# Sums of inputs for Strassen products in five steps, first group's products reordered, spectral split a row later

## The chip, the cores and the metric

One Trainium2 chip, of which the kernel uses one core. A core has engines with instruction queues of their own: TensorE (PE; its weight loads are shown as PEld), VectorE (DVE), ScalarE (ACT), GpSimd (POOL) and SyncE (SP), which here issues most of the transfers; 16 DMA engines move the data. The metric is device time in microseconds (us) of one execution, lower is better. Times are compared as medians of several runs.

## The reference

Two branches read the same layer-normalised input, and their sum is added to the input:

```python
x = A_u                                  # (1, 2048, 576)
xn = _layernorm(x, axis=-1)
return x + _A_ref(xn, ...) + _B_ref(xn, B_w1, B_w2)

# _A_ref: a state-space convolution over the sequence
logdA = dt * A;  dB = dt * Bc
P = jnp.exp(logdA[:, :, None] * l[None, None, :])
K = jnp.einsum("dn,dnl,dn->dl", Cc, P, dB).real     # 576 kernels of length 2048
...
Yf = Uf * Kf[None, :, :, :]                         # product of the two spectra
y = ... irfft ... + u * Dskip[None, None, :]

# _B_ref: a feed-forward layer, F = 4608
h = _silu(jnp.einsum("bsd,df->bsf", x, w1))
out = jnp.einsum("bsf,fd->bsd", h, w2)
```

## The kernel before

**Numbers.** Matrix products run on float32 values that are split into a high and a low part (names ending in h and l): three products, high by high, high by low and low by high, stand for one. The splits are a cast on ScalarE (h) and a subtraction on VectorE (l). An inner dimension of 576 is four tiles of 128 and a rest of 64, whose high and low parts share one tile of 128 rows (x4, x40, x41).

**The feed-forward branch** (`ffn`) sets the order of the program. The sequence has four blocks of 512 tokens, two to a half. A first matmul with w1 (`up`) makes 128 hidden features by 512 tokens, `gate`-like code applies SiLU and splits the result into gh and gl, and `down` multiplies 128 tokens of it with w2 into PSUM tiles po of 288 columns, which VectorE adds into the accumulators acc (L313). The first half, and two chunks of the second half, run block by block in that way (up to L418).

**The Strassen part** (`wino_ffn`, L421) does the rest of the second half. A group n (14 of them, `first` to `end`) is 256 hidden features (f = 2n and 2n + 1) by both blocks of 512 tokens, with the inner dimension halved into 2 x 256: a 2 x 2 by 2 x 2 product, made of seven products rather than eight, in the form with shared sums. `prod` is one such product, six matmuls of 512 columns; `rest` adds the rest of the inner dimension, two matmuls. On the weight side sums are made per group (`sums`, `prep`, `split`), named c1, c2, t13 and t24. On the input side they are made once, by `wino_x` (L548):

- `join` puts the halves of x together again (x21, x22, x11, x12: VectorE, 128 x 1024 each);
- S1 = x21 + x22, S2 = S1 - x11, S3 = x11 - x21, S4 = x12 - S2, each split by `parts` (ScalarE, then VectorE). S3 overwrites the tiles of x21's block;
- d4 is the difference of the two rests (tiles e and d).

A[0], A[1] and A22 are parts of the input that need no sum. `wino_x` makes S1, S2, S4 and d4, yields once, and makes S3.

In a group the PSUM tiles are pb (name pb or pb2), pc (`ps_c`) and pa (`ps_a`): c1·A[0] goes to pb and is copied to pa; t13·S1 and a rest go to pc, copied to the SBUF tile f5; t24·S2 is added on pb, and VectorE makes pc = pb + f5 (L504); t13·S3 is added on pb, and f5 = pb + f5 (L510). Then come two ends: `lower` (the gate of f5, the product t24·A22 on pb and its gate) and `upper` (c2·S4 on pc with its gate, c1·A[1] on pa with its gate). Which end runs first alternates with n, since the next group's `down` steps d[0] to d[3] need the block whose gates came first. Between the products stand the previous group's `down` steps and the weights' loads and splits (`second`, `prep`).

**The convolution branch** runs as a side program (`side`), woven into the main one: `weave` counts the main program's yields (276 steps) and lets the side program go on whenever the count has reached the fraction that it last yielded. First come the kernel's taps (`kgen`, up to 0.613), stored to d1k, then `wino_x` at 0.6215, then `spectral` between 0.6215 and marks[2] = 0.855, then `tail`. `spectral` has 32 rows. `front(k)` loads the row of the input (ur) and of the kernel (kr), splits both, multiplies each with a Fourier matrix (pu, pk), forms the complex product ka (VectorE, with copies by ScalarE, L870 to L879) and splits it to yh and yl (`split_of`); in the loop, `front(k + 1)` stands ahead of the last product of row k (tile pb of L892, from yh and yl), which is copied to yo and stored to d2. The memory of the kernel's taps (pool of `stage`), of `wino_x`'s sums and of the spectral rows is used one after the other.

**The end.** The convolution's output for 128 tokens (`add_conv`, tiles py) needs rows of d2 from all 32 spectral rows, so that its loads (ys, 32 of them) can begin only when the last row is stored; six of them are buffered at a time. r holds the first half's result, stored earlier in dr0 and loaded again; after the addition (L971) it is stored (L172).

**Who sets the order.** The text gives a priority by its order, and a scheduler with a time model of its own orders each engine's queue at build time; what is inside `high_priority` goes ahead, `behind(ins)` keeps an instruction after another of its engine. At run time each engine works its queue strictly in that order, and waits at the first instruction whose inputs or buffers are not ready. The lines that the change touches are L486 to L541 (the group), L548 to L588 (`wino_x`), L852 to L895 (`spectral`) and L1018 to L1024 (the fractions).

Of the kernel before, what the change touches and what calls it, by code (L numbers as in the profile page):

```python
# [41 lines left out]
def kernel(  # L42
# [21 lines left out]
    nc = tc.nc  # L64
# [25 lines left out]
    s4 = None  # L90
# [39 lines left out]
    xts = {}  # L130
    pairs = {}
    pins = {}
    wino = {}
# [287 lines left out]
    def wino_ffn(load_w1, load_w2, split_w2, prep, WT, first, end, W2, before, down):  # L421

        ps_a = ps1.tile([P, 512], F32, tag="ps1", name="pa")
        ps_c = ps1.tile([P, 512], F32, tag="ps1", name="pc")
        A, A22, S1, S2, S3, S4, x40, x41, d4 = wino["x"]
        nc.tensor.matmul(ps_a, x40[:, :P], x40, start=True, stop=True)
        G = {}

        def unit(name, n, a):
            h, l = WT[name, n]  # L430
            return h[:, a:a + 2], l[:, a:a + 2]

        def prod(dst, w, x, start=False, stop=False):
            (wh, wl), (xh, xl) = w, x
            n = 0
            for a, v in ((wh, xh), (wh, xl), (wl, xh)):
                for kt in range(2):
                    pins["pe"] = nc.tensor.matmul(dst, a[:, kt], v[:, kt], start=start and n == 0, stop=stop and n == 5,  # L438
                                                  skip_group_check=True).ins
                    n += 1  # L440

        def rest(dst, name, n, at, x4, stop=True):
            for i in range(2):
                pins["pe"] = nc.tensor.matmul(dst, WT[name, n][i][:, at], x4, start=False, stop=stop and i == 1,
                                              skip_group_check=True).ins

        def gate(src, b, f):
            gf = gp.tile([P, 512], F32, tag="gf", name="gf", bufs=2)
            spare = len(G) % 6 == 5
            gh, gl = ((wino["pool"] if spare else gp).tile([P, 512], F32R, tag=n, name=n) for n in ("gh", "gl"))  # L450
            G[b, f] = gh, gl
            with tc.high_priority():
                nc.scalar.activation(gf, src, AF.Silu)
                pins["gh"] = nc.scalar.copy(gh, gf).ins
                pins["gl"] = nc.vector.tensor_sub(gl, gf, gh).ins

        def load(n):
            if n < end:
                load_w1(1, n // 2, n % 2 * 2)

        def second(n, i, part):
            if first <= n < end:
                f = 2 * n + i
                (load_w2 if part == "load" else split_w2)(1, f // FT, f % FT)

        load(first + 1)
        for i in range(2):
# [12 lines left out]

        def run_of(b, ns):
            fs = [2 * n + i for n in ns for i in range(2)]
            blk = (1, NCH - 1 if ns[-1] == end - 1 else WINO_C, b)
            return [lambda jj=jj: down(blk, jj, [(G[b, f], W2[1, f // FT, f % FT]) for f in fs]) for jj in range(4)]

        for n in range(first, end):  # L486
            d = downs(n - 1)
            pb = ps2.tile([P, 512], F32, tag="ps2", name="pb2")
            f5 = wino["pool"].tile([P, 512], F32, tag="f5", name="f5", bufs=1)
            prod(pb, unit("c1", n, 0), A[0], start=True)  # L490
            with tc.high_priority():
                nc.scalar.copy(ps_a, pb)
            prod(ps_c, unit("t13", n, 0), S1, start=True)
            rest(ps_c, "c2", n, 2, x41)
            with tc.high_priority():
                nc.scalar.copy(f5, ps_c)
            yield 0
            d[0]()
            second(n, 0, "split")
            second(n + 1, 0, "load")  # L500
            yield 0
            prod(pb, unit("t24", n, 0), S2)
            with tc.high_priority():
                nc.vector.tensor_add(ps_c, pb, f5)  # L504
            d[1]()
            prep(n + 1, "c2")
            yield 0
            prod(pb, unit("t13", n, 2), S3)
            with tc.high_priority():
                nc.vector.tensor_add(f5, pb, f5)  # L510
            d[2]()
            prep(n + 1, "c1")
            prep(n + 1, "sums")
            yield 0
            d[3]()
            second(n, 1, "split")
            second(n + 1, 1, "load")
            yield 0

            def lower():  # L520
                gate(f5, 1, 2 * n + 1)
                prod(pb, unit("t24", n, 2), A22)
                gate(pb, 1, 2 * n)

            def upper():
                prod(ps_c, unit("c2", n, 0), S4)
                rest(ps_c, "c2", n, 2, d4)
                gate(ps_c, 0, 2 * n + 1)
                prod(ps_a, unit("c1", n, 2), A[1])
                rest(ps_a, "c1", n, 4, x40)  # L530
                gate(ps_a, 0, 2 * n)

            rest(pb, "c1", n, 4, x41, stop=False)
            for k, f in enumerate((lower, upper) if n % 2 == 0 else (upper, lower)):
# [12 lines left out]

    def wino_x(sx, xp):  # L548

        (ah, al, x40), (bh, bl, x41) = xts[2], xts[3]  # L550

        def join(h, l, k, name):
            t = sx.tile([P, 2, 512], F32, name=name)
            nc.vector.tensor_add(t, h[:, k:k + 2].bitcast(F32), l[:, k:k + 2].bitcast(F32))
            return t

        def parts(src, h, l):
            with behind(pins["gh"]):
                nc.scalar.copy(h, src)
# [9 lines left out]
        x21, x22 = join(bh, bl, 0, "x21"), join(bh, bl, 2, "x22")  # L569
        nc.vector.tensor_add(x22, x21, x22)  # L570
        S1 = parts(x22, *new("s1"))
        x11 = join(ah, al, 0, "x11")
        nc.vector.tensor_sub(x21, x11, x21)
        nc.vector.tensor_sub(x11, x22, x11)
        S2 = parts(x11, *new("s2"))
        x12 = join(ah, al, 2, "x12")
        nc.vector.tensor_sub(x12, x12, x11)
        S4 = parts(x12, *new("s4"))
        nc.vector.tensor_sub(e, x40.bitcast(F32), x41.bitcast(F32))
        nc.scalar.copy(e2[:64], e[64:])  # L580
        nc.vector.tensor_add(e[:64], e[:64], e2[:64])
        nc.scalar.copy(d4[:64], e[:64])
        nc.vector.tensor_sub(d4[64:], e[:64], d4[:64])
        yield 0
        S3 = parts(x21, bh[:, 0:2], bl[:, 0:2])
        wino["x"] = ([(ah[:, 0:2], al[:, 0:2]), (ah[:, 2:4], al[:, 2:4])], (bh[:, 2:4], bl[:, 2:4]),
                     S1, S2, S3, S4, x40, x41, d4)
        wino["pool"] = xp  # L588

    kl = yp = pa = tail_at = None  # L590
    kf = {}
# [260 lines left out]
    def spectral():  # L852
# [5 lines left out]
        def front(k):  # L858
            m3 = mats("m3", k, 2)
# [4 lines left out]
            ka = kl.tile([P, D], F32, tag="ka", name="ka")  # L864
# [12 lines left out]
                nc.vector.tensor_mul(kb[:64, hs], pu[64:, :HD], kb[:64, hs])  # L877
                nc.vector.tensor_mul(kb[64:, hs], pu[:64, :HD], kb[64:, hs])
            nc.vector.tensor_add(ka, ka, kb)  # L879
            return m3, split_of(ka, "y", 1)  # L880

        m2s = {0: mats("m2", 0, 0)}
        nxt = front(0)
        for k in range(32):
            m3, ys = nxt
            if k < 31:
                nxt = front(k + 1)
            yo = kl.tile([P, D], F32, tag="yo", name="yo")
# [88 lines left out]
    def side():  # L977
# [39 lines left out]

        xp = ctx.enter_context(tc.tile_pool(name="xp", bufs=1))  # L1018
        with tc.tile_pool(name="sx", bufs=1) as sx:
            for _ in wino_x(sx, xp):  # L1020
                yield 0.6215
        with tc.tile_pool(name="kl", bufs=1) as kl:
            for at in spectral():
                yield 0.6215 + (at - 1) * (marks[2] - 0.6215)  # L1024
        yp = ctx.enter_context(tc.tile_pool(name="yp", bufs=3))
        yield from tail()

# [88 lines left out]
```

## Time and profile before

| | us |
|---|---|
| Median of 3 runs | 1140.56 (1139.49 to 1141.24) |
| The profiled execution | 1145.05 |
| Its span, from the first to the last instruction | 1143.3 |
| Strassen part starts (dummy matmul, L426) | 664.1 |
| First and last store of a spectral row issued (L894) | 713.3 and 1067.5 |
| First and last ys load issued (L950) | 1070.6 and 1123.6 |

In the profile, a group of instructions reads: line, engine, operation, output tile <- input tiles, by the program's names with buffer numbers left out (d stands for d1u, d1k or d2, r for r0, x for x21 and the like). An engine is busy while an instruction of it runs. An idle time is put down to the instruction or transfer that ended it, the releaser: "<-DVE acc L313" means that the engine went on when that addition was done. Matmuls overlap, so the time of one is read from a run of several. PEclk is the clock that TensorE was granted, as a share of full speed. The DMA share is the mean busy share of the 16 DMA engines. In the chain of waits the end is followed backwards, at each step to what released it.

### The profile page before, as it was taken

To read this page: it belongs to the slowest core of one execution; us is meant where nothing else is said; L and a number is where in the kernel's file an instruction comes from. 1 tells how busy PE (TensorE), PEld (TensorE's weight loads), DVE (VectorE), ACT (ScalarE), POOL (GpSimd) and SP (SyncE) were. 2 spreads that over 40 slices of the span, in tenths; PEclk is the share of its full clock that TensorE was granted. 3 is DMA by queue.
4 is the path that set the end of the run, shared out by engine and by line. 5 is a ranking of instruction groups with operands and counts; after the bars stand their busy time and mean duration, and the time that the engine had idled before them with its cause. 6 is when DMAs were issued, how large, how long until landed. Compare 5 with 4: busy or idle time off the path is not lost.

```text
span 1143.3 us, 23137 instructions
## 1 busy us (share of the span) xinstructions
PE 1101.7 (96%) x9101; PEld 989.3 (87%) x9101; DVE 981.5 (86%) x1675; ACT 735.9 (64%) x1297; POOL 98.5 (9%) x178
## 2 busy tenths in 40 slices
PE   6999999999999999999999989999999999999878
PEld 5998998988889898898899977999899888999766
DVE  6698999999999999999999688998898779888535
ACT  4665557676667677667676437787878667877310
POOL 1001000000000000000000001111111111110012
PEclk9999999999999999999999999999999999999989
DMA  9456412424232525175924136445444445442697
GB/s 272 132 161 214 126 35 80 103 91 102 90 92 60 138 74 127 47 202 187 244 75 109 44 74 181 133 138 152 135 113 144 136 133 151 149 144 90 148 236 229
DMA packets 167372, 151.26 MB, mean 132 GB/s; under 512 B 87984, under 2 KB 136128, under 8 KB 166624
## 3 DMA queue, kind: packets, MB, share of 16 engines
q1 hardware_dynamic: 150128, 112.66, 35.8%
q0 software_dynamic: 16752, 36.24, 10.1%
q8 instruction: 72, 1.18, 0.4%
q10 hardware_dynamic: 384, 0.89, 0.3%
q14 instruction: 36, 0.29, 0.1%
HBM read 103.74 MB, written 46.08 MB: 131 GB/s over the span
## 4 chain that ended last, share of the span: by engine, by line
PE 59%; DVE 18%; DMA 9%; ACT 9%; issue 3%; SPq 1%; DVEq 0%; ACTq 0%
PE po L309 26%; PE ph L286 14%; PE pb L438 3%; DMA w1r<-in_B_w_dram 3%; PE kp L818 2%; DVE acc L313 2%; PE pc L438 2%; PE z L833 1%; PE ph L287 1%; PE ph L288 1%; PE pk L943 1%; DMA dxt<-xt 1%; PE pu L943 1%; DVE w1l L356 1%; PE pb L943 1%
## 5 line engine op out<-in xcount | busy, mean ns | idle before, releaser
L309 PE MATMUL po<-w2h,gh 128*128 128x288 f32 x1152 | 339.7, 299 | 7.5 <-DVE acc L313 5.4
L309 PE MATMUL po<-w2l,gh 128*128 128x288 f32 x1152 | 339.1, 297 | 0.4 <-DVE w2l L275 0.4
L309 PE MATMUL po<-w2h,gl 128*128 128x288 f32 x1152 | 336.1, 297 | 0.6 <-DVE gl L296 0.6
L309 PEld LDWEIGHTS po<-w2h,gh 128*128 128x128 f32 x1152 | 216.1, 189 | 21.8 <-DVE acc L313 8.4
L309 PEld LDWEIGHTS po<-w2l,gh 128*128 128x128 f32 x1152 | 216.9, 189 | 8.1 <-issue 2.3
L309 PEld LDWEIGHTS po<-w2h,gl 128*128 128x128 f32 x1152 | 215.5, 189 | 3.3 <-DVE gl L296 0.9
L313 DVE TENSOR_TENSOR acc<-po,acc 128x288 f32<-128x288 f32 x296 | 129.0, 450 | 29.0 <-PE po L309 27.5
L286 PE MATMUL ph<-xh,w1h 128*128 128x512 f32 (+1 forms) x368 | 99.4, 387 | 0.9 <-ACT xh L123 0.6
L286 PE MATMUL ph<-xl,w1h 128*128 128x512 f32 (+1 forms) x368 | 98.6, 383 | 0.0
L286 PE MATMUL ph<-xh,w1l 128*128 128x512 f32 (+1 forms) x368 | 97.3, 382 | 0.0
L294 ACT ACTIVATE gf<-ph 128x512 f32<-128x512 f32 (+1 forms) x92 | 52.9, 576 | 44.3 <-PE ph L288 26.8
L273 ACT CAST w2h<-w2r 128x576 fp32r<-128x576 f32 x72 | 47.7, 674 | 47.8 <-PE po L309 32.6
L286 PEld LDWEIGHTS ph<-xl,w1h 128*128 128x128 f32 x368 | 66.5, 189 | 12.4
L286 PEld LDWEIGHTS ph<-xh,w1l 128*128 128x128 f32 x368 | 66.6, 188 | 12.1
L286 PEld LDWEIGHTS ph<-xh,w1h 128*128 128x128 f32 x368 | 65.3, 191 | 11.0 <-ACT xh L123 0.9
L777 ACT ACTIVATE c<-th,magic 128x1040 f32<-128x1040 f32 x36 | 42.0, 1167 | 43.8 <-DVE C L798 34.1
L296 DVE TENSOR_TENSOR gl<-gf,gh 128x512 fp32r<-128x512 f32 (+1 forms) x92 | 60.5, 659 | 8.8 <-ACT gh L295 8.4
L779 ACT ACTIVATE c<-th 128x1040 f32<-128x1040 f32 x36 | 38.7, 1074 | 37.9 <-DVE th L778 37.8
L295 ACT CAST gh<-gf 128x512 fp32r<-128x512 f32 (+1 forms) x92 | 55.3, 602 | 7.7 <-PE po L309 6.4
L855 POOL DMA_DIRECT2D m<-in_cm_dram x64 | 34.5, 540 | 295.8 <-PE pu L943 196.1
L157 POOL DMA_DIRECT2D d1u<-u x32 | 17.4, 542 | 451.6 <-ACT u L156 451.6
L275 DVE TENSOR_TENSOR w2l<-w2r,w2h 128x576 fp32r<-128x576 f32 x72 | 53.5, 749 | 2.0 <-ACT w2h L273 1.8
(268 smaller groups left out, 2449.6 us busy)
## 6 DMA issues: line engine op xcount, KB each, us to landing
w2r<-in_B_w_dram SPq DMA_DIRECT2D x72, 288.0 KB, 3.9
w1r<-in_B_w_dram SPq DMA_DIRECT2D x35, 512.0 KB, 3.8
d1u<-u POOLq DMA_DIRECT2D x32, 288.0 KB, 2.7
d1k<-stage SPq DMA_DIRECT2D x18, 512.0 KB, 7.2
ur<-d1u SPq DMA_DIRECT2D x32, 288.0 KB, 3.0
kr<-d1k SPq DMA_DIRECT2D x32, 288.0 KB, 2.8
d<-yo POOLq DMA_DIRECT2D x32, 288.0 KB, 2.8
ys<-d SPq DMA_DIRECT2D x32, 288.0 KB, 9.6
```

Source lines behind the costliest of these rows:

```text
L273: pins["w2h"] = nc.scalar.copy(h2, r2).ins
L275: nc.vector.tensor_sub(l2, r2, h2)
L286: nc.tensor.matmul(ph, w[:, kt, :], v[:, kt, a:e], start=n + kt == 0, stop=False)
L294: nc.scalar.activation(gf, ph, AF.Silu)
L295: pins["gh"] = nc.scalar.copy(gh, gf).ins
L296: pins["gl"] = nc.vector.tensor_sub(gl, gf, gh).ins
L309: pins["pe"] = nc.tensor.matmul(po[:, :HD], gs[g][:, js], ws[w][:, hs], start=n == 0, stop=n == 3 * len(terms) - 1).ins
L313: nc.vector.tensor_add(acc[j][:, hs], po[:, :HD], acc[j][:, hs])
L438: pins["pe"] = nc.tensor.matmul(dst, a[:, kt], v[:, kt], start=start and n == 0, stop=stop and n == 5, skip_group_check=True).ins
L777: nc.scalar.activation(c65, th, AF.Identity, bias=magic)
L779: nc.scalar.activation(c65, th, AF.Abs)
L855: nc.gpsimd.dma_start(m, cm23[:, k, i:i + 2])
```

## The change

In three parts: the products of a group become small functions, and for the first group they are called in another order (c1·A[0], then c1·A[1] with its gate, and only then those with S1, S2, S3; its ends are c2·S4 and then t24·A22). `wino_x` is cut into five steps, one main step apart, with the names of its tiles set ahead of the first, and the two token blocks change roles. In `spectral` the split of row k's product is issued when the loop comes to row k, not at the end of `front(k)`. The spectral rows start at step 176 of 276 (0.6377) where it was 0.6215 (step 171.5), and end at the same fraction.

```diff
@@ wino_ffn, in the loop over groups
-            prod(pb, unit("c1", n, 0), A[0], start=True)
-            with tc.high_priority():
-                nc.scalar.copy(ps_a, pb)
-            prod(ps_c, unit("t13", n, 0), S1, start=True)
-            rest(ps_c, "c2", n, 2, x41)
...
+            def p1():
+                prod(pb, units["c1", n, 0], A[0], start=True)
+                with tc.high_priority():
+                    nc.scalar.copy(ps_a, pb)
+
+            def p5():
+                prod(ps_c, units["t13", n, 0], S1, start=True)
+                rest(ps_c, "c2", n, 2, x41)
+                with tc.high_priority():
+                    nc.scalar.copy(f5, ps_c)
...
+            def c11():
+                prod(ps_a, units["c1", n, 2], A[1])
+                rest(ps_a, "c1", n, 4, x40)
+                gate(ps_a, 1, 2 * n)
+
+            def c12():
+                prod(ps_c, units["c2", n, 0], S4)
                 rest(ps_c, "c2", n, 2, d4)
-                gate(ps_c, 0, 2 * n + 1)
...
+                gate(ps_c, 1, 2 * n + 1)
+
+            def c2x():
+                gate(f5, 0, 2 * n + 1)
+                prod(pb, units["t24", n, 2], A22)
+                gate(pb, 0, 2 * n)
+
+            def c1x():
+                c12()
+                c11()
...
+            if n == first:
+                order = ((p1, 0), (c11, 1), (2,), (p5, p6, 3), (p7,))
+                ends = c12, c2x
+            else:
+                order = ((p1, p5), (0,), (p6, 1), (p7, 2), (3,))
+                ends = (c1x, c2x) if n % 2 == 0 else (c2x, c1x)
+            for steps in order:
+                for f in steps:
+                    if callable(f):
+                        f()
+                    else:
+                        d[f]()
+                        side_w(f)
+                yield 0
@@ wino_x
-        (ah, al, x40), (bh, bl, x41) = xts[2], xts[3]
+        (ah, al, x40), (bh, bl, x41) = xts[3], xts[2]
...
         x21, x22 = join(bh, bl, 0, "x21"), join(bh, bl, 2, "x22")
+        S1, S2, S4 = new("s1"), new("s2"), new("s4")
+        S3 = bh[:, 0:2], bl[:, 0:2]
+        wino["x"] = (...)
+        wino["pool"] = xp
+        yield 0
         nc.vector.tensor_add(x22, x21, x22)
-        S1 = parts(x22, *new("s1"))
+        parts(x22, *S1)
+        yield 0
         x11 = join(ah, al, 0, "x11")
         nc.vector.tensor_sub(x21, x11, x21)
         nc.vector.tensor_sub(x11, x22, x11)
-        S2 = parts(x11, *new("s2"))
+        parts(x11, *S2)
+        yield 0
+        parts(x21, *S3)
         x12 = join(ah, al, 2, "x12")
         nc.vector.tensor_sub(x12, x12, x11)
-        S4 = parts(x12, *new("s4"))
+        yield 0
+        parts(x12, *S4)
...
@@ spectral
-            return m3, split_of(ka, "y", 1)
+            return m3, ka
...
         for k in range(32):
-            m3, ys = nxt
+            m3, y = nxt
+            ys = split_of(y, "y", 1)
             if k < 31:
                 nxt = front(k + 1)
@@ side
-            for _ in wino_x(sx, xp):
-                yield 0.6215
+            for k, _ in enumerate(wino_x(sx, xp)):
+                yield (171 + k) / 276
         with tc.tile_pool(name="kl", bufs=1) as kl:
             for at in spectral():
-                yield 0.6215 + (at - 1) * (marks[2] - 0.6215)
+                yield 176 / 276 + (at - 1) * (marks[2] - 176 / 276)
```

The numbers 0 to 3 in `order` are the previous group's `down` steps with the loads and splits that stand beside them (`side_w`): 0 and 3 the w2 split and load (`second`), 1 the split of c2 for the next group, 2 that of c1 and its sums.

More of the change, by code (lines that the diff above doesn't have):

```diff
@@ L489, in wino_ffn @@
             f5 = wino["pool"].tile([P, 512], F32, tag="f5", name="f5", bufs=1)
-            prod(pb, unit("c1", n, 0), A[0], start=True)
-            with tc.high_priority():
-                nc.scalar.copy(ps_a, pb)
-            prod(ps_c, unit("t13", n, 0), S1, start=True)
-            rest(ps_c, "c2", n, 2, x41)
[L495 to L526, printed above, removed]
-                rest(ps_c, "c2", n, 2, d4)
-                gate(ps_c, 0, 2 * n + 1)
-                prod(ps_a, unit("c1", n, 2), A[1])
-                rest(ps_a, "c1", n, 4, x40)
-                gate(ps_a, 0, 2 * n)
+            units = {k: unit(*k) for k in (("c1", n, 0), ("c1", n, 2), ("t13", n, 0), ("t13", n, 2),
+                                           ("t24", n, 0), ("t24", n, 2), ("c2", n, 0))}
@@ new lines, in p1, with p6 @@
+            def p1():
[7 more added lines that the diff above has]
+                    nc.scalar.copy(f5, ps_c)
+            def p6():
+                prod(pb, units["t24", n, 0], S2)
+                with tc.high_priority():
+                    nc.vector.tensor_add(ps_c, pb, f5)
@@ new lines, in p7 @@
+            def p7():
+                prod(pb, units["t13", n, 2], S3)
+                with tc.high_priority():
+                    nc.vector.tensor_add(f5, pb, f5)
+            def c11():
[4 more added lines that the diff above has]
+                prod(ps_c, units["c2", n, 0], S4)
+                rest(ps_c, "c2", n, 2, d4)
+                gate(ps_c, 1, 2 * n + 1)
[3 more added lines that the diff above has]
+                gate(pb, 0, 2 * n)
@@ new lines, in c1x, with side_w @@
+            def c1x():
+                c12()
+                c11()
+            def side_w(k):
+                if k == 0:
+                    second(n, 0, "split")
+                    second(n + 1, 0, "load")
+                elif k == 1:
+                    prep(n + 1, "c2")
+                elif k == 2:
+                    prep(n + 1, "c1")
+                    prep(n + 1, "sums")
+                elif k == 3:
+                    second(n, 1, "split")
+                    second(n + 1, 1, "load")
@@ L533, in wino_ffn @@
             rest(pb, "c1", n, 4, x41, stop=False)
-            for k, f in enumerate((lower, upper) if n % 2 == 0 else (upper, lower)):
+            for k, f in enumerate(ends):
                 f()
@@ L569, in wino_x @@
         x21, x22 = join(bh, bl, 0, "x21"), join(bh, bl, 2, "x22")
+        S1, S2, S4 = new("s1"), new("s2"), new("s4")
+        S3 = bh[:, 0:2], bl[:, 0:2]
+        wino["x"] = ([(ah[:, 0:2], al[:, 0:2]), (ah[:, 2:4], al[:, 2:4])], (bh[:, 2:4], bl[:, 2:4]),
+                     S1, S2, S3, S4, x40, x41, d4)
+        wino["pool"] = xp
+        yield 0
         nc.vector.tensor_add(x22, x21, x22)
-        S1 = parts(x22, *new("s1"))
+        parts(x22, *S1)
+        yield 0
         x11 = join(ah, al, 0, "x11")
@@ L584, in wino_x @@
         yield 0
[L585 to L588, printed above, removed]
     kl = yp = pa = tail_at = None
```

## The prediction

> **What bounds the kernel now.** I read the profile page first, then TensorE's waits from the start of the Strassen part, busy time by stretches, the chain of waits near the end, and instructions in order of time around two places. The built orders of both kernels' instructions, in which no time stands, give the counts.
>
> ```profile
> span 1143.3 us, 23137 instructions
> PE 1101.7 (96%) x9101; PEld 989.3 (87%) x9101; DVE 981.5 (86%) x1675; ACT 735.9 (64%) x1297; POOL 98.5 (9%) x178
> ```
>
> TensorE is the bound: 41.6 us of idle time in 1143.3. The profiled execution took 1145.05 us, 1.75 more than its span and 4.5 more than the runs' median of 1140.56; I work out a difference from its trace and add it to the median. From 664 us on, the waits are these (engine, line, releaser: us in total, times, longest):
>
> ```profile
> PE py L964 <- DMA ys<-d: 8.9, 3, 3.1
> PE po L309 <- DVE acc L313: 3.8, 3, 2.7
> PE pu L943 <- ACT kb L873: 2.6, 1, 2.6
> PE pb L438 <- ACT s2h L559: 1.3, 1, 1.3
> ```
>
> There are two knots. One is the first Strassen group, with waits of 2.66, 1.26 and 2.60 us. The other is the end, where the convolution's last matmuls (py) wait 8.9 us for rows (ys) that may be loaded only when the last spectral row is stored.
>
> ```profile
> 1075.70 11.35 DMA r<-dr
> 1087.06 11.29 DMA ys<-d
> ...
> 1070.60:1111.60 41.00, 32.07 (x223) 23.46 (x222) 12.04 (x25) 5.76 (x11) 3.91 (x8) 0.92 1.01 245
> 1111.60:1116.50 4.90, 4.90 (x53) 4.09 (x53) 3.06 (x8) 0.34 (x1) 0.03 (x1) 1.00 0.03 9
> 1116.50:1132.00 15.50, 14.87 (x184) 11.58 (x184) 8.03 (x21) 0.00 (x0) 5.79 (x12) 1.00 1.01 292
> 1132.00:1143.30 11.30, 6.25 (x68) 5.27 (x68) 5.63 (x14) 0.00 (x0) 0.97 (x2) 0.94 0.59 177
> ```
>
> The first two rows are pieces of the chain of waits (start, length, what): 22.6 us of the end hang on transfers. In the others, after start and end, stand the length, busy time of PE, PEld, DVE, ACT and POOL, granted clock, DMA share, GB/s. For 41 us the DMA engines are full (1.01) while TensorE works 32; then they do nothing for 4.9; then they are full again for 15.5.
>
> **The change part by part.** Every engine has the same instructions in the same number before and after: nothing is added or removed, only order moves. GpSimd's order is unchanged; on SyncE, loads of spectral rows move among weight loads, and the convolution's loads stay behind them all.
>
> *Products that need no sum first.* TensorE's order does not differ at all until 75 matmuls after the start of the Strassen part (L426), apart from which token block is read. Before the change the product c1·A[1] already stood ahead of the first product with S1. So this part moves little there; what it moves is VectorE's and ScalarE's order.
>
> ```profile
> 668.00:684.00 16.00, 12.05 (x76) 10.33 (x75) 15.94 (x23) 6.31 (x8) 0.00 (x0) 1.00 0.07 19
> 665.10 4.63 DVE L554 TENSOR_TENSOR x<-xh,xl 128x1024 f32<-128x1024 f32 x4 [0.45 <-DMA d1k<-stage]
> 671.39 0.45 DVE L313 TENSOR_TENSOR acc<-po,acc 128x288 f32<-128x288 f32 x1
> 671.89 0.40 PE L309 MATMUL po<-w2h,gh 128*128 128x288 f32 x1 [2.66 <-DVE acc L313]
> 680.34 0.73 PE L438 MATMUL pb<-s2h,w1h 128*128 128x512 f32 x2 [1.26 <-ACT s2h L559]
> 684.76 0.45 DVE L313 TENSOR_TENSOR acc<-po,acc 128x288 f32<-128x288 f32 x1
> 685.21 0.70 DVE L504 TENSOR_TENSOR pc<-pb,f 128x512 f32<-128x512 f32 x1
> 686.32 0.76 DVE L275 TENSOR_TENSOR w2l<-w2r,w2h 128x576 fp32r<-128x576 f32 x1 [0.41 <-ACT w2h L273]
> 686.61 0.63 PE L438 MATMUL pb<-xh,w1h 128*128 128x512 f32 x2
> 691.38 0.68 DVE L455 TENSOR_TENSOR gl<-gf,gh 128x512 fp32r<-128x512 f32 x1
> ```
>
> VectorE sets this stretch: 15.94 us of 16 busy. In its new order the four joins (4.63 us, whose start waits for a store that shares their memory) still stand ahead of the first acc, so most of the 2.66 us wait stays. Up to pc<-pb at 685.21 the new order has the same work plus three instructions that today come later: a gl (0.68, the early gate), a w2l (0.76) and an acc (0.45), together 1.9 us. So pc<-pb would start at 687.1 and end at 687.8. The products with S3 accumulate into the bank that it reads and wait for it; behind them in TensorE's queue stand those with S4 and A22. They start at 687.8 instead of 686.61: a loss of 1.2 us, in which I count the waits before it, since these only change places ahead of a full VectorE.
>
> ```profile
> 697.01 0.40 PE L943 MATMUL pu<-uh,m 128*128 128x288 f32 x1 [2.60 <-ACT kb L873]
> 696.00:704.00 8.00, 6.80 (x31) 6.12 (x32) 7.28 (x14) 7.79 (x17) 0.54 (x1) 0.79 0.23 57
> 1061.11 3.18 PE po L309 x24
> 1108.10 1.36 PE pb L438 x6
> ```
>
> The 2.60 us wait for ScalarE's copies gains. Between the products pk and the one that waits today the new order puts 21 other matmuls: 11 of 288 columns at 3.18/24 = 0.1325 us and 10 of 512 at 1.36/6 = 0.227, together 3.7 us, enough to hide it. The clock of 0.79 over these 8 us costs 1.7; I take half of it as gone, since other waits remain. Gain at the start: 2.6 + 0.85 - 1.2 = 2.2 us. Its bounds are 8.2 (2.66 + 1.26 + 2.60 + 1.7, all gone) and -1.2 (the cover fails).
>
> *Spectral rows later.* They begin at step 176 instead of 171.5 and the split of y is issued a row later. Counted from the start of the Strassen part in TensorE's order, the first spectral output product has 22 more matmuls of 288 columns and 14 more of 512 ahead of it (2.9 + 3.2 = 6.1 us), the last one 48 and 38 more (6.4 + 8.6 = 15.0 us). The first 6.1 come from the later start; the other 8.9 build up over 31 rows. Up to there the cover is complete: TensorE simply does other work first. But the last row is what the end waits for:
>
> ```profile
> 1066.41 0.29 PE L943 MATMUL pb<-yh,m 128*128 128x288 f32 x1
> 1067.51 0.54 POOL L894 DMA_DIRECT2D d<-yo  x1 [4.51 <-ACT yo L893]
> 1070.59 0.62 SPq L950 DMA_DIRECT2D ys<-d  x1
> ```
>
> Last product, store, first ys load, 4.2 us apart in all. The first ys load moves from 1070.6 by 15.0 - 2.2 = 12.8 us to 1083.4; behind it in SyncE's queue stand all other ys loads and the r loads, for which the last py, the last sums and the output wait.
>
> *How long the end then takes.* Its transfers (KB each, us to landing):
>
> ```profile
> ys<-d SPq DMA_DIRECT2D x32, 288.0 KB, 9.6
> r<-dr SPq DMA_DIRECT2D x4, 576.0 KB, 8.1
> out_dram<-r POOLq DMA_DIRECT2D x16, 144.0 KB, 6.9
> out_dram<-acc POOLq DMA_DIRECT2D x6, 144.0 KB, 5.0
> out_dram<-acc SPq DMA_DIRECT2D x6, 144.0 KB, 4.9
> out_dram<-acc SPq DMA_DIRECT2D x4, 72.0 KB, 2.3
> out_dram<-acc ACTq DMA_DIRECT2D x4, 72.0 KB, 2.4
> ...
> SPq L950 <- PE py L964: 15.0, 4, 9.1
> 1119.54 1.19 PE py L964 x31
> ```
>
> 16128 KB, or 16.5 MB, none of which can start before the last row. At the full share these are 41.0 + 15.5 + 11.3 x 0.59/1.01 = 63.1 us. TensorE's work after the last row shrinks from 240 matmuls of 288 columns, 51 of 512 and 128 py to 192, 13 and 128: 25.4 + 3.0 + 9.5 (16 py, recorded twice each, in 1.19 us) = 38 us. Today's 4.9 us without transfers came when SyncE waited for py to free a row's buffer (15.0 us in four waits), py standing behind other matmuls; with 38 us of work beside 63 of transfers I take this as gone. The end lasts 72.7 - 4.9 = 67.8 us; with the taper of the last stretch gone as well, 63.1; with the gap kept, 72.7.
>
> Sum: 15.0 - 2.2 - 4.9 = +7.9 us, so 1140.56 + 7.9 = 1148.5 (span 1151.2). The extremes are 15.0 - 8.2 - 9.6 = -2.8 and 15.0 + 1.2 = +16.2.
>
> **The rivals.**
>
> *TensorE at half clock in the end* (slower still). For it speaks this row, which follows waits of 3.05 and 2.97 us:
>
> ```profile
> 1098.00:1104.00 6.00, 5.52 (x28) 3.44 (x29) 0.46 (x1) 0.67 (x1) 0.00 (x0) 0.50 1.07 290
> ```
>
> With 30 us of idle time in the new end, all its 38 us could run at 0.50: 76 us, and 15.0 - 2.2 + 3.3 = +16.1, 1156.7. It decides from 67.8 us on, when four fifths of the work run so. Against it: 0.92 over today's 41 us, with 9 idle. The Trainium skill (TensorE: Matmul & The Clock Gate, Part 1) says that the clock is halved after an idle window of about 3.4 us and restored after one of sustained work; the 0.50 agrees, and by that rule waits of that length spread over the new end would bring this rival's 1156.7.
>
> *The start is recovered whole.* The joins are now spread over steps, and all of 8.2 us goes: 15.0 - 8.2 - 4.9 = +1.9, 1142.5. Against it: joins still stand ahead of acc, and VectorE is full.
>
> *The late row is hidden anyway.* Matmuls only change sides of the last row, and the end shrinks by the 15 us of work that left it: -2.2, 1138.4. For it: TensorE was the bound overall. Against it: share 1.01 where TensorE has idle time.
>
> *The end's transfers run faster throughout* (faster). At 292 GB/s, the rate of the second full stretch, from the first load to the last store, 16.5 MB take 56.5 us: 15.0 - 2.2 - 16.2 = -3.4, 1137.2. It decides below 57.6 us for the end (287 GB/s). Against it: 245 for 41 us with full engines, when small loads prevail. The Trainium skill (DMA: Bandwidth & Descriptors, Specifications) gives some 358 GB/s as a core's limit to HBM; an estimate by that page is 46 us, but no row of several microseconds here comes near it.
>
> *The change does not do what it says*: the order shows it for the products at the start, as counted above; that is in the forecast.
>
> **How the numbers follow.** What a measurement of this kernel can tell from no change is about 0.2%, 2.3 us: faster is below 1138.3, slower above 1142.8. Forecast 0.50 (its own range 1144 to 1153.5), half clock 0.12, start whole 0.14, hidden 0.14, faster transfers 0.10. Slower: 0.50 + 0.12 + 0.06 of the third (it lies near the bound) = 0.68. Faster: 0.10 + 0.07 of the fourth = 0.17. Same: 0.08 + 0.07 = 0.15. The range from 1138 to 1153.5 leaves out most of half clock and half of faster transfers, under 0.2.
>
> **What would show it.** Right: TensorE's wait for the first acc of the group still near 2 us; pc<-pb near 687; no 2.6 us wait for kb; the last d<-yo issued near 1080 instead of 1067.5; a DMA share near 1 from there to about 1140, with no gap; the span's end 66 to 70 us after the first ys load. Wrong: a last d<-yo before 1073 (the order does not set the time), an end under 60 us after it (TensorE, not transfers, sets it), or waits above 5 us anywhere between 700 and 1067.

## The result, and the profile after

The changed kernel takes 1147.41 us (median of 5 runs, 1145.25 to 1150.92) against 1141.24 for the kernel before on the same chip (5 runs, 1139.49 to 1142.84): a ratio of 1.0048 (95% interval 1.0028 to 1.0067), slower by half a per cent.

The page's first lines, the waits of TensorE from the start of the Strassen part (engine, line, releaser: us in total, times, longest), and the instructions that the prediction named, in order of time:

```profile
span 1145.6 us, 23130 instructions
PE 1101.8 (96%) x9101; PEld 992.5 (87%) x9101; DVE 980.5 (86%) x1675; ACT 736.9 (64%) x1297; POOL 98.4 (9%) x178
```

```profile
PE py L998 <- DMA ys<-d: 10.0, 5, 3.7
PE py L998 <- issue: 4.7, 2, 3.8
PE po L309 <- DVE acc L313: 4.2, 4, 2.2
PE pb L438 <- DVE pc L507: 2.8, 3, 1.4
PE pu L977 <- ACT kb L906: 0.4, 1, 0.4
```

```profile
672.07 0.40 PE L309 MATMUL po<-w2h,gh 128*128 128x288 f32 x1 [2.20 <-DVE acc L313]
...
687.41 0.69 DVE L507 TENSOR_TENSOR pc<-pb,f 128x512 f32<-128x512 f32 x1
...
688.16 0.72 PE L438 MATMUL pb<-xh,w1h 128*128 128x512 f32 x2 [1.40 <-DVE pc L507]
...
1073.91 0.29 PE L977 MATMUL pb<-yh,m 128*128 128x288 f32 x1
...
1075.26 0.54 POOL L928 DMA_DIRECT2D d<-yo  x1 [6.68 <-ACT yo L927]
...
1078.34 0.62 SPq L984 DMA_DIRECT2D ys<-d  x1
```

In the first group the wait for acc has become 2.20 us where it was 2.66, the wait for s2h is gone, the wait of 2.60 us for kb has become 0.4, and a new one of 1.40 us stands ahead of the products with S3. The last spectral row's store comes 7.75 us later (1075.26 against 1067.51), and the first ys load as much. The end after it takes 1145.6 - 1078.3 = 67.3 us where it took 72.7. Together that is 7.75 - 5.4 = +2.3 us, the difference of the two profiled spans. The medians differ by 6.2, because the profiled execution of before (1145.05) lay 3.8 over the median of these runs, while that of after is the median. The spans therefore place the gains and losses, and the ratios give their size. The same holds for the experiments below: a profile is of one execution, and these lay up to 4.3 us from the median of their kernel (e3 4.3 under it, e2 3.4 over it, e4 3.1 under it).

Busy time by stretches, before in the first two rows, then after (start, end, length; busy PE, PEld, DVE, ACT, POOL; granted clock, DMA share, GB/s):

```profile
820.00:940.00 120.00, 118.31 (x736) 107.80 (x735) 102.03 (x194) 89.07 (x190) 16.25 (x31) 1.00 0.47 141
940.00:1060.00 120.00, 119.08 (x745) 109.17 (x744) 103.94 (x199) 93.21 (x199) 15.70 (x29) 1.00 0.42 127
```

```profile
668.00:684.00 16.00, 12.97 (x79) 10.93 (x78) 15.94 (x24) 7.05 (x10) 0.00 (x0) 1.00 0.09 23
696.00:704.00 8.00, 7.29 (x44) 6.46 (x44) 6.52 (x13) 7.82 (x18) 0.54 (x1) 1.00 0.32 91
820.00:940.00 120.00, 119.69 (x762) 111.21 (x761) 104.75 (x202) 92.65 (x199) 16.78 (x31) 1.00 0.49 141
940.00:1060.00 120.00, 120.00 (x763) 111.57 (x762) 104.21 (x198) 94.06 (x198) 16.76 (x31) 1.00 0.46 134
1078.30:1116.50 38.20, 28.02 (x206) 20.61 (x204) 9.22 (x19) 4.64 (x8) 3.90 (x8) 0.84 1.02 251
1118.00:1120.00 2.00, 1.64 (x24) 0.80 (x24) 1.38 (x5) 0.00 (x0) 0.00 (x0) 0.50 0.04 15
1120.00:1122.00 2.00, 2.00 (x39) 1.31 (x40) 1.52 (x5) 0.00 (x0) 1.64 (x4) 0.50 0.44 100
1116.50:1132.00 15.50, 11.45 (x134) 7.31 (x134) 8.86 (x22) 0.00 (x0) 5.80 (x12) 0.74 0.83 259
1132.00:1145.60 13.60, 7.66 (x94) 6.21 (x94) 5.75 (x14) 0.00 (x0) 0.97 (x2) 0.98 0.70 221
```

VectorE still fills the start (15.94 of 16 us). In the 240 us from 820 on TensorE issues 44 more matmuls in the same time and at the same clock. The DMA engines are still full in the end (share 1.02 for 38 us), and it still has a hole in them near 1118 to 1122, shorter than the 4.9 us of before.

For the comparison of kernels below I split the time from the start of the Strassen part to the last spectral product in two. The *work* is the matmuls issued between, at 0.1325 us for 288 columns and 0.2275 for 512; the *lost time* is the rest, waits and low clock together. (The median distance from start to start is 0.133 and 0.231 us in these traces. With those, all lost times are about 3 us less, and their differences stay.) Before: 664.09 + 381.43 + 20.89 = 1066.41. After: 664.73 + 396.44 + 12.74 = 1073.91. The change puts 15.0 us more work ahead of the last row and loses 8.1 us less time. By stretches the lost time is, before and after: to 700 us 9.1 and 5.8; 700 to 820, 3.7 and 4.7; 820 to 1060, 7.9 and 2.1.

### The profile page after: what moved, and what is told of

Same layout as the page of the kernel before. It is cut to its first block, busy times and chain, and to the rows that moved or that the text cites. A ratio compares the mean times of both kernels' runs of the same rounds, so it can differ in the third digit from the quotient of the medians.

```text
span 1145.6 us, 23130 instructions
## 1 busy us (share of the span) xinstructions
PE 1101.8 (96%) x9101; PEld 992.5 (87%) x9101; DVE 980.5 (86%) x1675; ACT 736.9 (64%) x1297; POOL 98.4 (9%) x178
## 4 chain that ended last, share of the span: by engine, by line
PE 73%; DVE 11%; DMA 8%; ACT 4%; issue 3%; SPq 1%; DVEq 0%; POOL 0%; ACTq 0%; POOLq 0%
PE po L309 31%; PE ph L286 16%; PE pb L438 5%; PE pc L438 3%; DMA ys<-d 2%; PE kp L851 2%; PE pb L977 2%; PE pu L977 2%; PE pk L977 2%; PE pa L438 1%; PE ph L287 1%; DVE acc L313 1%; DMA w1r<-in_B_w_dram 1%; PE ph L288 1%; PE z L866 1%
## 5 line engine op out<-in xcount | busy, mean ns | idle before, releaser
L286 PEld LDWEIGHTS ph<-xh,w1l 128*128 128x128 f32 x368 | 67.1, 190 | 12.1
```

What stands on the lines that cost most here:

```text
L286: nc.tensor.matmul(ph, w[:, kt, :], v[:, kt, a:e], start=n + kt == 0, stop=False)
```

## The experiments

Three parts of the change show in the engines' order: the exchange of the token blocks' roles, the first group's new order of products, and the later split of y. (Taken out of the changed kernel, the steps of `wino_x` alter four places of VectorE's built order and nothing else, and the fraction at which the spectral rows start alters nothing in any engine's built order.) Five runs take the parts one by one; then come the end, and what sets the place of the last row.

**e1: the exchange alone, in the kernel before.**

```diff
 def lower():
-    gate(f5, 1, 2 * n + 1)
+    gate(f5, 0, 2 * n + 1)
...
-    for k, f in enumerate((lower, upper) if n % 2 == 0 else (upper, lower)):
+    for k, f in enumerate((upper, lower) if n % 2 == 0 else (lower, upper)):
...
-    (ah, al, x40), (bh, bl, x41) = xts[2], xts[3]
+    (ah, al, x40), (bh, bl, x41) = xts[3], xts[2]
```

> The kernel before with one part of the change alone: the two token blocks exchange roles in the Strassen part, so that the other end of each group runs first. Its built order puts 10.0 us more matmul work ahead of the last spectral product than before (the whole change puts 15.0). Theory of the last row (the end follows the first load of convolution rows, about 67 us later): last spectral row stored 4 to 10 us later than 1067.5, time +2 to +5 us (1.002 to 1.005). Rival (TensorE's own waits in the first group and between set the time, the last row is hidden): within 1 us of before unless its first-group waits differ from 6.5 us, and then by that difference.

Measured: 1.0101 (1.0079 to 1.0122). That is slower than the theory had it (1.002 to 1.005) and far from the rival. The work ahead of the last row rises by 10.0 us as counted, and the lost time by 4.4, which neither expectation held:

```profile
1081.94 0.54 POOL L894 DMA_DIRECT2D d<-yo  x1 [3.62 <-ACT yo L893]
```

The store is 14.4 us later than before. An exchange that removes and adds no instruction puts the last row two thirds as far back in TensorE's program as the whole change does: the 15 us were not the later start and the later split, as I had them. At the start this kernel gains: the wait for kb is gone (the trace shows none there), and to 700 us it loses 5.0 us where before loses 9.1. Between 700 and 1060 it loses 20.1 where before loses 11.6.

**e2: the split of y back in front, in the changed kernel.**

```diff
-            return m3, ka
+            return m3, split_of(ka, "y", 1)
...
-            m3, y = nxt
-            ys = split_of(y, "y", 1)
+            m3, ys = nxt
```

> The changed kernel with the split of y put back into the front of a row (role exchange and product order kept). Its built order has 1.9 us less matmul work ahead of the last spectral product than the changed kernel. Theory of the last row: 0 to 2 us faster than the changed kernel, so 1.003 to 1.005 of before. Rival (holding ka until the next row costs by itself, 0.29 us in each of 31 rows, the 8.9 us that the prediction put on the rows): 6 to 9 us faster than the changed kernel, at or below before.

Measured: 1.0080 (1.0062 to 1.0098), slower than the changed kernel, where both expectations had it faster. The work is 1.9 us less, but the lost time goes from 12.7 to 19.0 (in an execution 3.4 us over its median), and the last store comes at 1081.79. In this company the later split gains, by some 0.3%; the two intervals just overlap.

**e3: the first group in the order of all others, in the changed kernel.**

```diff
-            if n == first:
-                order = ((p1, 0), (c11, 1), (2,), (p5, p6, 3), (p7,))
-                ends = c12, c2x
-            else:
-                order = ((p1, p5), (0,), (p6, 1), (p7, 2), (3,))
-                ends = (c1x, c2x) if n % 2 == 0 else (c2x, c1x)
+            order = ((p1, p5), (0,), (p6, 1), (p7, 2), (3,))
+            ends = (c1x, c2x) if n % 2 == 0 else (c2x, c1x)
```

> The changed kernel with the first group's products in the order of the other groups (role exchange and late split kept). 4.5 us less matmul work ahead of the last spectral product than in the changed kernel. Theory of the last row: 2 to 4 us faster than the changed kernel if the first group's waits stay as they are (about 4.3 us). Rival (the new product order is what gained at the start): the waits of the first group go back to about 6.5 us with the clock drop, and the time is within 1 us of the changed kernel or slower.

Measured: 1.0098 (1.0078 to 1.0119), slower, as only the rival allowed, with 4.5 us less work ahead of the last row and 9.0 us more lost time. But the rival's reason does not hold either. The start loses nothing by the old order (5.0 us to 700, 5.8 in the changed kernel); what is lost lies between 700 and 1060 (16.6 against 6.8).

**e4: the later split alone, in the kernel before** (the edit of e2 the other way round).

> The kernel before with the split of y issued a row later, and nothing else. 1.2 us more matmul work ahead of the last spectral product. Theory of the last row: +0 to +1.5 us. Rival (the late split alone costs 0.29 us a row): +6 to +9 us. A third possibility, that the late split takes waits out of the rows between 700 and 1060 us (the changed kernel lost 5 us less there): -2 to -5 us.

Measured: 1.0038 (1.0025 to 1.0051), 4.4 us, which lies between the expectations. The work rises by 1.2 us, the lost time stays (20.8), the last product comes 1.1 us later and the last store 3.0. Alone, the later split loses a little.

**e9: the exchange undone, in the changed kernel**; the new order and the later split stay (the edit of e1 the other way round, in the new functions).

> The changed kernel with the exchange of the sums' roles undone; the first group's new order of products and the later split of y stay. Theory (the matmul work that stands ahead of the last spectral row in TensorE's program sets the end): 394.5 us of it stand ahead here against 396.4 in the changed kernel and 381.4 in the kernel before; with the exchange gone the first product comes earlier but the start's losses come back (9 us as before, against 5.8), so the last row lands 1 us earlier to 3 us later than in the changed kernel, and the ratio to before is 1.003 to 1.008. Rival (the exchange itself is what costs, as the exchange alone with 1.010 hints): the ratio is 1.000 or less.

Measured: 1.0105 (1.0079 to 1.0131), outside both expectations. The work is as counted (394.4 us, 2.0 under the changed kernel), but the lost time is 21.5 instead of 12.7: 1.7 us more at the start and 7.0 more between 700 and 1060. I had expected it back at the start alone.

The five runs and the two kernels together (x marks a part that is in; times in us):

| Kernel | exchange | new order | late split | work | lost | last store | ratio |
|---|---|---|---|---|---|---|---|
| before | | | | 381.4 | 20.9 | 1067.51 | 1 |
| e4 | | | x | 382.6 | 20.8 | 1070.49 | 1.0038 |
| e1 | x | | | 391.4 | 25.3 | 1081.94 | 1.0101 |
| e3 | x | | x | 391.9 | 21.7 | 1078.16 | 1.0098 |
| e9 | | x | x | 394.4 | 21.5 | 1081.06 | 1.0105 |
| e2 | x | x | | 394.5 | 19.0 | 1081.79 | 1.0080 |
| after | x | x | x | 396.4 | 12.7 | 1075.26 | 1.0048 |

The parts don't add. With the exchange or the new order in, 10 to 13 us more work stands ahead of the last row, and with both only 13 to 15; the lost time falls far only with all three. A second execution of either kind says the same, so that this is hardly the scatter of single profiles: e5 below, in which TensorE has the order of before up to the last row, loses 22.9 us, and e6, the changed kernel without the last row, 13.7. The new order without both other parts was not run. The ratio goes roughly with the last store.

**e5: what a late last row costs.** In the kernel before, the last row goes to DRAM and back ahead of its store.

```diff
+            if k == 31:
+                nc.gpsimd.dma_start(dhop, yo)
+                nc.gpsimd.dma_start(yo, dhop)
             nc.gpsimd.dma_start(d2.rearrange("(p k) d -> k p d", k=32)[k], yo)
```

> The kernel before, with the last spectral row sent through DRAM and back before it is stored, so that only that store comes later, by two transfers of about 2.8 us: 5.5 to 6.5 us. TensorE does the same work. Theory of the last row: the first load of convolution rows moves from 1070.6 to about 1076.5, and the time rises by 3 to 6 us. Rival (the late row is hidden behind TensorE's work): within 1 us of before.

Measured: 1.0034 (1.0021 to 1.0048).

```profile
1070.78 0.54 POOL L896 DMA_DIRECT2D dhop<-yo  x1 [4.21 <-ACT yo L894]
1073.93 0.55 POOL L897 DMA_DIRECT2D yo<-dhop  x1 [2.61 <-DMA dhop<-yo]
1077.17 0.54 POOL L898 DMA_DIRECT2D d<-yo  x1 [2.69 <-DMA yo<-dhop]
...
1080.09 1.29 SPq L954 DMA_DIRECT2D ys<-d  x2
```

The two transfers hold the last store back by 6.4 us (1070.78 to 1077.17). The first ys load is 9.5 us later (1080.09 against 1070.59); the other 3 us were lost ahead of the last row, in the same order of matmuls, and belong to this execution. The span is 4.8 us longer and the median 0.34% or 3.9 us, so the late row is not hidden, and the end gives back a part, from 72.7 to 68.0 us. How much it gives back by itself this run can't tell, because the edit moved something else too: behind the last row TensorE's order is another, and 16.0 us of other matmuls stand between the last spectral product and the first inverse step (py) where before has 10.2.

**e6: the last row earlier.** The changed kernel without the loads, products and split of the last spectral row; the product of row 30 is stored in its place.

```diff
-        for k in range(32):
+        for k in range(31):
...
             nc.gpsimd.dma_start(d2.rearrange("(p k) d -> k p d", k=32)[k], yo)
+            if k == 30:
+                nc.gpsimd.dma_start(d2.rearrange("(p k) d -> k p d", k=32)[31], yo)
```

> The changed kernel without the work of the last spectral row (row 30's product is stored in its place as well): 18 matmuls, 2.4 us of TensorE, are left out, and the last store comes about a row's interval, 7 to 11 us, earlier. Theory of the last row: 5 to 10 us faster than the changed kernel. Rival (TensorE's work sets the end): 2.4 us faster.

Measured: 0.9916 (0.9904 to 0.9929).

```profile
1064.86 1.28 SPq L986 DMA_DIRECT2D ys<-d  x2
```

The first ys load comes 13.5 us earlier than in the changed kernel (1078.34); the span is 12.8 us shorter, and the end takes 67.9 us. That is more than the 5 to 10 us expected, and far more than the 2.4 us of work left out. With the first ys load at 1065, 1078 or 1080 (e6, after, e5) the end takes 67.9, 67.3 and 68.0 us. Over all nine kernels with one buffer for ka this load comes between 1065 and 1085 and the end takes 67.3 to 72.7 us, without a trend: the time follows the last row.

**e7 and e8: a buffer more for ka.** In `spectral`, ka gets two buffers, so that a row need not wait until the one before it is split; m3 gives one up to make room. e7 is this edit in the kernel before, e8 in the changed one.

```diff
-            m = kl.tile([P, 2, P], F32R, tag=name, name=name, bufs=2)
+            m = kl.tile([P, 2, P], F32R, tag=name, name=name, bufs=1 if name == "m3" else 2)
...
-            ka = kl.tile([P, D], F32, tag="ka", name="ka")
+            ka = kl.tile([P, D], F32, tag="ka", name="ka", bufs=2)
```

> The kernel before with two buffers for ka instead of one, paid for with one buffer less for the matrix m3. In its built order the last spectral product has 23.8 us less matmul work ahead of it than before. Theory of the last row: the last row is stored before 1050, transfers of the end begin while TensorE still has some 67 us of other matmuls, its 8.9 us of waits for ys go, and the time falls by 5 to 12 us. Rival (the last row does not matter): within 1.5 us of before.

> The changed kernel with two buffers for ka and one for m3. 40.0 us less matmul work ahead of the last spectral product than in the changed kernel. Theory of the last row: it is stored near 1035, the waits for ys at the end go, and the time is 10 to 18 us below the changed kernel, below before as well, by 4 to 12 us, and at or below the kernel before with two buffers, by what the first group gains (0 to 4 us). Rival: within 1.5 us of the changed kernel.

Measured: e7 1.0031 (1.0019 to 1.0043), slower where 5 to 12 us of gain were expected; e8 0.9963 (0.9951 to 0.9975), faster than both kernels, at the lower edge of what was expected, though its waits for ys did not go. The work ahead of the last row falls to 358 and 356 us, the last stores to 1048.31 and 1040.38. But the ends take 95 us: the rule that the time follows the last row is left. In e7 the last row is 19 us earlier than before and the kernel is slower. In e8, the waits of TensorE from 1040 on are one line, and these are its places (in order of time, idle time in brackets):

```profile
1051.25 0.72 PE L998 MATMUL py<-ys,s 64*32 64x288 f32 x16 [0.61 <-DMA ys<-d]
1055.29 0.69 PE L998 MATMUL py<-ys,s 64*32 64x288 f32 x8 [2.32 <-DMA ys<-d]
...
1065.12 0.84 PE L998 MATMUL py<-ys,s 64*32 64x288 f32 x16 [1.91 <-DMA ys<-d]
...
1074.35 1.33 PE L998 MATMUL py<-ys,s 64*32 64x288 f32 x16 [4.23 <-DMA ys<-d]
...
1084.30 0.69 PE L998 MATMUL py<-ys,s 64*32 64x288 f32 x8 [1.11 <-DMA ys<-d]
```

The inverse steps now stand so close behind the last row that TensorE, in its fixed order, waits 10.2 us in all for rows to land, while other matmuls are queued behind them: in the built order the first inverse step stands 368.0 us of work behind the start, the last spectral row 356, and the whole without the inverse steps is 425.

**e10, e11 and e12: the inverse steps later in the plan.** e8 with other fractions for the tail; the numbers are those of e10, e11 has 0.950 and 0.0040, e12 0.930 and 0.0045.

```diff
-        tail_at = (0.895, 0.0055, 0.919, 0.0052)
+        tail_at = (0.895, 0.0055, 0.940, 0.0045)
```

> The changed kernel with two ka buffers and one m3 buffer (which alone gave 0.9963 of before), and with the tail's inverse steps due later in the plan, so that the first stands 376.4 us of matmul work behind the start instead of 368.0. Theory: the 10.2 us that TensorE waited for ys between 1050 and 1084 go for the most part, and the span falls by 4 to 8 us: 0.989 to 0.993 of before. Rival: the six ys buffers are held longer, the last ten loads of y start later still, and the end is bound by the transfers again: 0.996 or more.

> As the run before it, with the first inverse step 378.7 us of matmul work behind the start. Theory: within 0.2% of that run, 0.988 to 0.994 of before. Rival (buffers held longer decide): slower than that run by more than 0.2%, because the loads of y that wait for a free buffer start later by the 2.3 us and by what this adds up to.

> The changed kernel with two ka buffers and one m3 buffer, and the tail's inverse steps spread closer in the plan with the first of them where it stood (368.0 us of matmul work behind the start). Theory: the waits for ys between 1050 and 1084 stay at about 10 us, so the ratio is that of the buffers alone, 0.995 to 0.998. Rival: closer steps free the ys buffers sooner, and the loads land earlier: 0.990 to 0.994.

Measured: e10 0.9916 (0.9896 to 0.9936), e11 0.9917 (0.9897 to 0.9936), e12 0.9971 (0.9956 to 0.9986). TensorE's waits from 1040 on in e10, all of them, and two stretches of its end:

```profile
PE po L309 <- DVE acc L313: 4.8, 1, 4.8
```

```profile
1060.00:1080.00 20.00, 15.22 (x112) 11.56 (x111) 11.22 (x23) 8.30 (x15) 1.97 (x4) 0.91 1.00 232
1080.00:1100.00 20.00, 20.00 (x171) 16.01 (x171) 8.64 (x20) 2.41 (x4) 3.87 (x8) 1.00 1.04 271
```

No wait for ys is left, and from 1080 on the transfers run beside a full TensorE. The one wait of 4.8 us in its place was not worked on. In the chain of waits (start, length, what) a load of w1 stands ahead of it, among the ys loads that fill the DMA engines:

```profile
1057.07 9.81 DMA w1r<-in_B_w_dram
1069.73 3.17 PE po L309 x12
```

e10 and e11 are the same within 0.2%, so later than e10 gains nothing; e12, whose first inverse step stands where e8 has it, is as fast as e8. (Its waits for ys are not the 10 us expected but 4.0; in their place py waits 3.7 us for an addition on r by VectorE and 0.8 for a load of r, and po 1.0 for acc: 9.5 in all.) What gains is the 8 us more of other matmuls between the last row and the first inverse step, not the closer steps. e10 is the best version of the study, 10 us under the kernel before (1135.08 against 1145.15 in the same comparison).

## Why the prediction was right or wrong

The predicted 1148.5 us, slower, stands against 1147.41. The path was right: more matmuls ahead of the last spectral row, a later first ys load, a somewhat shorter end. That the number is this close is in part luck, as the sum at the end of this list shows. Step by step:

- *The bound of the end* was right. e5 and e6 move the last row by transfers and by leaving a row out, neither without moving other matmuls, and the time follows it as long as the first ys load comes at 1065 or later. e7 to e12 show where this stops: with that load at 1044 to 1051, TensorE's waits and its own work decide.
- *The start* was right in its mechanisms: joins still ahead of acc, pc<-pb at 687.41 (predicted 687.1), the products with S3 at 688.16 (687.8), the wait for kb hidden. The clock term was taken as half gone and is gone whole (1.00 over 696 to 704, where it was 0.79). The gain to 700 us is 9.1 - 5.8 = 3.3 us, predicted 2.2; counted over the first 50 us of the Strassen part it is 9.9 - 8.3 = 1.6, since small waits now lie behind 700. The forecast put the hidden kb wait under the new order of products. It doesn't need that: with the exchange alone (e1) the wait is gone too.
- *The later last row* was mis-sized. Predicted 12.8 us, measured 7.75. The count of work was right (15.0 us); the term that was missing is the lost time from 700 to 1060 us, taken as unchanged, which fell by 4.9 us (11.6 to 6.8). What it consists of stays open: of the 7.9 us lost before between 820 and 1060 the profile lists 2.3 as waits, of the 2.1 after 0.3. e2, e3 and e9, each without one part of the change, lose 12.1, 16.6 and 13.8 us from 700 to 1060, so the fall came with all three parts only.
- *The cause of the 15 us* was wrong. "The first 6.1 come from the later start; the other 8.9 build up over 31 rows" named the start fraction and the late split. The fraction changes no engine's order, the split alone adds 1.2 us (e4). The exchange alone adds 10.0 (e1), and the new order with the split 13.0 (e9). Why the scheduler then puts more products ahead of the spectral rows was not tried.
- *The end's length* was right at 67.3 us (predicted 67.8), for a reason that is only half right. The hole in the transfers did not go: 2 us at a share of 0.04 and 2 at 0.44 are left of 4.9 us. The rest came from a full stretch of 38.2 us at 251 GB/s where it was 41.0 at 245, and a last stretch at a share of 0.70 where it was 0.59.
- *Half clock in the end*: there in part. The clock is 0.84 and 0.74 in the two stretches from 1078 to 1132, and 0.50 in the rows near 1120, behind waits of 3.8 us (no releaser shown) and 3.7 (for ys). The halving after waits of that length agrees with the Trainium skill (TensorE: Matmul & The Clock Gate, Part 1), cited in the prediction. An earlier half clock, from about 1090 to 1101, stands behind waits of 0.85 and 1.32 us only. It was not free: in the chain of waits (start, length, what) it lies right ahead of a load that the end hangs on, and 23 matmuls take 5.45 us there, where at 0.1325 each they would take 3.0. But the end took 67.3 us, not the rival's 76.

```profile
1092.00:1094.00 2.00, 2.00 (x12) 1.11 (x5) 0.00 (x0) 0.00 (x0) 1.90 (x4) 0.50 1.10 218
```

```profile
1095.81 5.45 PE po L309 x23
...
1102.64 11.03 DMA ys<-d
```

- *The other rivals* fell. The start was not recovered whole (3.3 of 8.2 us); the late row was not hidden (in e5, where the store is held back by 6.4 us, the time rises by 3.9); the transfers did not run at 292 GB/s throughout.
- *The sum*: 7.75 - 5.4 = +2.3 us by the traces, +7.9 predicted, +6.2 by the medians. That the forecast lies closer to the median than its own terms do is luck in part: the term of the last row (12.8) was 5 us too large, and the profiled execution of before, against which the sum was made, lay 3.8 us over its median. A single profile of this kernel is uncertain by that much.

## What to carry to other kernels

Where one late instruction releases the last transfers, count the matmul work that stands ahead of it in the built order, edit by edit: an exchange of two equal blocks that adds nothing moved it by 10 us here, and two parts that alone lose 0.4 and 1.0% cost 0.5% together with the third, so they must be measured in company as well as alone. Where such an instruction is brought forward (the second buffer of ka), what follows it has to be planned anew: work that has just been released must not stand straight behind its release on an engine with a fixed order, and 8 us more of other matmuls between the two (20.0 instead of 11.5) brought 0.5% (e8 to e10).

## What the runs showed of the hardware

How long TensorE waits does not by itself tell whether its clock is halved. In the kernel before, the clock fell behind a wait of 2.60 us (for kb, ended at 697.01) and stayed low for about 3 us; a wait of 2.66 us (for acc, ended at 671.89) in the same execution was followed by none. In e1 a wait of 1.82 us (for acc, ended at 707.52) was enough. The first two rows are of before, the others of e1:

```profile
672.00:673.00 1.00, 1.00 (x8) 1.00 (x9) 1.00 (x2) 0.00 (x0) 0.00 (x0) 1.00 0.89 249
699.00:700.00 1.00, 1.00 (x6) 1.00 (x5) 0.94 (x3) 0.98 (x3) 0.00 (x0) 0.50 0.61 131
706.00:707.00 1.00, 0.00 (x0) 0.00 (x0) 1.00 (x2) 0.00 (x0) 0.00 (x0) 1.00 0.66 170
708.00:709.00 1.00, 1.00 (x6) 0.83 (x5) 1.00 (x3) 0.68 (x2) 0.00 (x0) 0.50 0.95 265
```

And the core's transfers came to 346 GB/s over 4 us in the end of the changed kernel, beside 231 GB/s in another 4 us of the same end with equally full DMA engines. The prediction had set the 358 GB/s of the Trainium skill (DMA: Bandwidth & Descriptors, Specifications) aside because no row of several microseconds came near it; this one does, though no long stretch:

```profile
1104.00:1108.00 4.00, 2.61 (x28) 1.95 (x28) 0.28 (x1) 0.00 (x0) 1.03 (x3) 1.00 1.08 231
...
1126.00:1130.00 4.00, 4.00 (x34) 3.35 (x30) 2.88 (x7) 0.00 (x0) 1.82 (x4) 1.00 1.07 346
```
